# Taking temporaries and output pieces by the age of their store, and four lower halves on VectorE

## The chip, the cores and the metric

The kernel runs on one core of a Trainium2 chip. The metric is the device time of one execution in microseconds: the median of 3 runs of the kernel before is 1347.68 us (1347.32 to 1349.24).

## The reference

Chunked attention, then two feed-forward experts, all in float32. The second expert is the part that the change touches: `h = x @ w_in` with 4608 tokens, 512 to 2048 columns, then SiLU, then `@ w_out` back to 512.

```python
def _moe2_ref(x, w_in, w_out):
    h = x @ w_in
    g = h * (1.0 / (1.0 + np.exp(-h)))
    return (g @ w_out).astype(np.float32)

x = attention(q, k, v)          # chunks of 64, softmax, 8 heads
x = _moe_ref(x, moe_w_in, moe_w_out, moe_g_ln)   # SoLU and layer norm between two products
return _moe2_ref(x, moe2_w_in, moe2_w_out)
```

## The kernel before

One plan holds the work of all engines: `at(when, fn, ...)` puts a function at due times in us, and `Plan.run` calls the functions in order of due time. A function that yields goes on at its next due time. What is issued in this order stands in the same order in each engine's queue; an instruction that waits holds everything behind it on its engine. All DMAs are issued by SP, in order.

Every float32 product is made of three fp32r products of a high part and a lower part (`PASSES`): the high part is a rounded copy, the lower part is the value less that copy.

Both products of the second expert are done by blocks of 2 x 2 with seven products of half size (`SEVEN`: p1, p6, p2, p7, p5, p4, p3) in place of eight, and sums around them.

*Way in* (lines 478 to 630). A unit `u` is 768 tokens by two pieces of 128 hidden columns; the units are worked in 24 pairs, 14 products of 6 matmuls a pair, due `PA = 14 * SL = 14.59` us apart with `SL = 1.042`. The outputs are copied or summed out of PSUM into temporaries (`tmp`, 128 x 384): `c_p1` takes one, `c_u2` (line 598), `c_u3` (602) and `c22` (612) take one each, and the blocks c11, c22, c21 and c12 end in the pieces of p1, c22, u3 and u2. Each passes through SiLU on ScalarE and goes to DRAM (`gd`) by `g_store`. There are nine temporaries; `take()` hands them out in rotation. In one pair starting at x, unit i (0 or 1), the due times are y = x + (i + 1) SL + 0.05 for `c_p1`, y + 2 SL for `c_u2`, y + 6 SL for `c_u3`, y + 8 SL for `c22`; the stores are due at y + 4 SL + 0.8 (c11), y + 8 SL + 1.2 (c22), y + 10 SL + 1.2 (c21) and y + 12 SL + 1.2 (c12). A PSUM bank that a sum reads is written again by a later product, so a late sum stops TensorE: p7 goes into the bank that `c_u2` reads, p3 into the one that `c22` reads.

Beside it weights are prepared: `conv_a` (lines 159, 162), `conv_b` and `w2_mix` (250, 254 on GpSimd, stored at 257) make the second weight's pieces; `w2t` and `w2o` are loads of finished weights; `raw_load` (513) loads the input `ry` of the next 768 tokens, four loads of 384 KB, into five places, and `s_split` (548) cuts it into halves.

*Way out* (lines 633 to 735). Token pairs `v` of 256 tokens, 18 of them, seven products of 24 matmuls each. `g_load` (676) brings the rows from `gd` into one of two sets, `g_sum` (683) makes the sums, `g_split` makes the high part on ScalarE (694) and the lower part (696) on VectorE for the first four products and on GpSimd for the last three, into a ring of six places. Pairs 0 and 1 run interleaved (`turn`). `g_load(2, i)` overwrites the set that pair 0 read. Outputs are summed in six pieces (`ob`, line 721) and stored (734); `o_take` hands the pieces out by a table, in pairs from 2 on by a rotation of six.

Of the kernel before, what the change touches and what calls it, by code (L numbers as in the profile page):

```python
# [9 lines left out]
F32 = mybir.dt.float32  # L10
# [5 lines left out]
ALU = mybir.AluOpType  # L16
# [8 lines left out]
class Plan:  # L25
# [9 lines left out]
    def at(self, when, fn, *args):  # L35
        lead = self.lead.get((fn.__name__, *(a for a in args if isinstance(a, int))))
        when = [x / 100 for x in lead] if lead else [when] if isinstance(when, float) else when
        self.items.append((when, fn, args))
# [13 lines left out]
def chunk_attention_moe_moe(ctx: ExitStack, tc: tile.TileContext, q, k, v, w_in, w_out, g_ln, w2_in, w2_out, out):  # L52
    nc = tc.nc
# [54 lines left out]
    for i in range(2 * KD):  # L108
        kk, c = i % KD, i // KD * CW
# [3 lines left out]
    for m in range(KD):  # L113
        for a in range(2):
            src = w_out[a * 512:(a + 1) * 512, m * 128:(m + 1) * 128].rearrange("(k p) f -> p k f", p=128)
# [370 lines left out]
    wt, tu, raw_y, sy, bank, tmp, c_t = {}, [], {}, {}, {}, [], {}  # L486
# [65 lines left out]
        tmp.extend(t[:, i, 0:HW] for i in range(n))  # L552

    def take():
        tmp.append(tmp.pop(0))
        return tmp[-1]

    PLACE = {"p1": "x", "p2": "x", "p6": "y", "p7": "y", "p5": "w", "p3": "w", "p4": "v"}

# [25 lines left out]
    def g_store(u, half, low, c):  # L585
        p, j = divmod(u, NF)
        if p == NGR - 1:
            j = NF - 2 - j // 2 * 2 + j % 2
        t = GT * p + GT // 2 * half
        nc.sync.dma_start(out=gd[t:t + GT // 2, :, j + NF * low, :].rearrange("t p c -> p t c"), in_=c.rearrange("p (t c) -> p t c", c=128))  # L590

    def c_p1(u):
        c_t[u, "p1"] = c = take()
        nc.scalar.activation(out=c, in_=bank[u, "x"], func=AF.Copy)

    def c_u2(u):
        c_t[u, "u2"] = c = take()
        nc.vector.tensor_tensor(out=c, in0=bank[u, "y"], in1=c_t[u, "p1"], op=ALU.add)  # L598

    def c_u3(u):  # L600
        c_t[u, "u3"] = c = take()
        nc.vector.tensor_tensor(out=c, in0=bank[u, "y"], in1=c_t[u, "u2"], op=ALU.add)

    def c11(u):
        c = c_t[u, "p1"]
        nc.scalar.activation(out=c, in_=bank[u, "x"], func=AF.Silu)
        yield
        g_store(u, 0, 0, c)

    def c22(u):  # L610
        c = take()
        nc.vector.tensor_tensor(out=c, in0=bank[u, "w"], in1=c_t[u, "u3"], op=ALU.add)  # L612
        yield
        nc.scalar.activation(out=c, in_=c, func=AF.Silu)
        yield
        g_store(u, 1, 1, c)

    def c21(u):
        c = c_t[u, "u3"]
        nc.vector.tensor_tensor(out=c, in0=bank[u, "v"], in1=c, op=ALU.add)  # L620
        yield
        nc.scalar.activation(out=c, in_=c, func=AF.Silu)
        yield
        g_store(u, 0, 1, c)
# [9 lines left out]


    NP = TT // 2
    wo2, wu, ring, raw_g, ob, takes, o_t = {}, [], [], {}, [], [], {}

    def w2o_load(tag, bufs, n):

# [46 lines left out]
    def turn(v, o):  # L687

        return 7 * v + o if v > 1 else ((0, 1, 3, 5, 7, 9, 11), (2, 4, 6, 8, 10, 12, 13))[v][o]

    def g_split(v, o):
        src = raw_g[v % 2, G_FROM[SEVEN[o]]]
        dst = ring[turn(v, o) % 6]
        nc.scalar.activation(out=dst[:, 0], in_=src, func=AF.Copy)  # L694
        yield
        (nc.gpsimd if o > 3 else nc.vector).tensor_tensor(out=dst[:, 1], in0=src, in1=dst[:, 0].bitcast(F32), op=ALU.subtract)  # L696

    def out_product(v, o):
        acc, start = place(1000 + v, SEVEN[o], 256)
# [5 lines left out]

    def o_take(v, name):

        if v < 2:
            n = {"p1": (0, 2), "u2": (1, 3), "u3": (4, 0), "c22": (5, 2)}[name][v]
        else:  # L710
            n = (1, 4, 5, 2, 0, 3)[len(takes) % 6]
            takes.append(n)
        o_t[v, name] = ob[n]
        return ob[n]

    def o_p1(v):
        nc.scalar.activation(out=o_take(v, "p1"), in_=bank[1000 + v, "x"], func=AF.Copy)  # L717

    def o_sum(v, name, src, with_, new):
        c = o_take(v, name) if new else o_t[v, with_]  # L720
        nc.vector.tensor_tensor(out=c, in0=bank[1000 + v, src], in1=o_t[v, with_], op=ALU.add)  # L721
        if name[0] == "c":
            yield
            o_store(v, int(name[1]) - 1, int(name[2]) - 1, c)

    def o_c11(v):
        c = o_t[v, "p1"]
        nc.scalar.activation(out=c, in_=bank[1000 + v, "x"], func=AF.Copy)
        yield
        o_store(v, 0, 0, c)  # L730

    def o_store(v, i, n, c):
        b, tt = divmod(2 * v + i, BT)
        nc.sync.dma_start(out=out.rearrange("(b s) f -> b s f", b=B)[2 * tt:2 * tt + 2, b * CH:(b + 1) * CH, 256 * n:256 * n + 256], in_=c)


    plan = Plan(LEAD)
# [11 lines left out]
    for i in range(2 * KD):  # L749
        at((-70.0 if i < 4 else -69.0) + 0.1 * i, conv_load, i)  # L750
        x = -31.0 + 2.6 * i
# [11 lines left out]
    for t in range(TT):  # L763
        x = T[t]
# [22 lines left out]
        if t >= BT:  # L787
            x, (b, m) = T[t], divmod(t - BT, BT)
            y = (11.7, 16.9, 19.8)
            if t + 2 == TT:  # L790
                y = (11.7, L + 9.0, L + 11.8)
            elif t + 1 == TT:
                y = (12.0, 15.0, 17.8)
# [3 lines left out]
        x = T[t]  # L797
        for _ in range(CONV[t] if nxt < N1 else 0):
            at(x - 13.5, conv_load, nxt)
            x = T[t] + (3.6 if nxt == 18 else 0.0)  # L800
# [4 lines left out]
            else:  # L805
                at(x + 5.2, conv_c, nxt, side(nxt))
                if nxt % 2:
                    y = 122.2 if nxt == 17 else x + 5.3
# [6 lines left out]
    for m in range(KD):  # L815
        x = XO + 5.44 * m
# [5 lines left out]
    PA = 14 * SL  # L822
    BUFS = {"kT": 1, "pT": 1, "qT": 1, "e": 1, "xs": 1, "wi": 2 * KD, "wo": 4}
    UNITS = {"qT": 1, "e": 1, "wo": 4}
    for when, tags in (
# [5 lines left out]
        for i, tag in enumerate(tags):  # L831
            n = UNITS.get(tag, 2)
# [13 lines left out]
    for n in range(NGR * NF // 2):  # L846
        x = XA + PA * n
        p, jj = divmod(n, NF // 2)
        for i in range(2):
            u = 2 * n + i  # L850
            for o, name in enumerate(SEVEN):
                at(x + (2 * o + i) * SL, product, u, name)
            y = x + (i + 1) * SL + 0.05
            at(y, c_p1, u)
            at(y + 2 * SL, c_u2, u)
            at((y + 4 * SL, y + 4 * SL + 0.8), c11, u)
            at(y + 6 * SL, c_u3, u)
            at([y + 8 * SL + d for d in (0.0, 0.6, 1.2)], c22, u)
            at([y + 10 * SL + d for d in (0.0, 0.6, 1.2)], c21, u)
            at([y + 12 * SL + d for d in (0.0, 0.6, 1.2)], c12, u)  # L860
        if jj == 0:
            x -= PA
            on = ((ACT, DVE), (ACT, DVE), (ACT, DVE), (ACT, DVE), (ACT, POOL), (ACT, DVE), (ACT, POOL))
            for o, (hi_on, lo_on) in enumerate(on):
                y = x + (2 * o + 2) * SL + 0.2
                if p == 0:
                    y = XO + 1.0 + 2.0 * o if o < 5 else XA + 0.3 + 1.2 * o - 6.0
                at((y, y + 1.0), s_split, p, o, hi_on, lo_on)
                if o in (0, 2):
                    at(y + 1.1, raw_t, p, 2 if o == 0 else 3)  # L870
            if p + 1 < NGR:
                y = x + PA * (2.7 if p == 0 else 1.5)
                for i, q4 in enumerate((1, 0, 2, 3)):
                    at(y + 0.7 * i, raw_load, p + 1, q4)
                at(x + PA * (3.75 if p % 2 == 0 else 2.8), raw_t, p + 1, 0)
                at(x + PA * (3.9 if p % 2 == 0 else 2.93), raw_t, p + 1, 1)

    before = XA - 6.3
    for i in range(K2):
        n = N1 + i  # L880
        x = XA + PA * (8 * (i // 6) + ((0.7, 1.4, 2.4, 4.3, 5.4, 6.1) if i < 6 else (0.4, 1.1, 2.2, 2.85, 5.4, 6.1))[i % 6])
# [10 lines left out]
    for when, step, tags in (  # L892
# [5 lines left out]
        for tag in tags:  # L898
            n = UNITS.get(tag, 2)
# [13 lines left out]
    for vp in range(NP):  # L913
        x = XB + 7 * SB * vp
        for i in (2, 3, 0, 1):
            at(XB + FIRST_LOADS[vp][i] if vp < 3 else x - 11 * SB + 0.1 * i, g_load, vp, i)
        for n in range(4):
            at(XB + FIRST_SUMS[vp][n] if vp < 2 else x + (-6.2, -5.7, -3.2, -0.9)[n] * SB, g_sum, vp, n)
        ends = []
        for o in range(7):  # L920
            n = turn(vp, o)
            y = XB + (FIRST_SPLITS[n] if n < 14 else (n - 4.7) * SB)
            at((y, y + 1.25), g_split, vp, o)
            at(XB + n * SB, out_product, vp, o)
            ends.append(XB + n * SB + SB)
        d = 0.6 if vp == NP - 1 else 3.4
        at(ends[0], o_p1, vp)
        at(ends[1], o_sum, vp, "u2", "y", "p1", 1)
        at((ends[2], ends[2] + d), o_c11, vp)
        at(ends[3], o_sum, vp, "u3", "y", "u2", 1)  # L930
        at((ends[4], ends[4] + d), o_sum, vp, "c22", "w", "u3", 1)
        at((ends[5], ends[5] + d), o_sum, vp, "c21", "v", "u3", 0)
        at((ends[6], ends[6] + d), o_sum, vp, "c12", "w", "u2", 0)
# [161 lines left out]
```

## Time and profile before

| | |
|---|---|
| median of 3 runs | 1347.68 us |
| the profiled execution | 1346.99 us, span 1345.2 us |
| busy: PE, DVE, ACT, POOL | 95%, 67%, 45%, 42% of the span |
| way in of the second expert on PE | 589.9 to 965.3 us |
| way out on PE | 965.3 us to the end |
| mean granted TensorE clock | 0.988 |
| `gd<-tmp` stores (192 KB) | 192 |

PE is the matrix engine, PEld its weight load, DVE is VectorE, ACT ScalarE, POOL GpSimd, SP the engine that issues DMAs. Times in the rows are us from the start of the span. A bracket at the end of a row is the idle time of the engine before it, and who ended it. A row with a count merges instructions that follow each other.

### The profile page before, as it was taken

To read this page: it belongs to the slowest core of one execution; us is meant where nothing else is said; L and a number is where in the kernel's file an instruction comes from. 1 tells how busy PE (TensorE), PEld (TensorE's weight loads), DVE (VectorE), ACT (ScalarE), POOL (GpSimd) and SP (SyncE) were. 2 spreads that over 40 slices of the span, in tenths; PEclk is the share of its full clock that TensorE was granted. 3 is DMA by queue.
4 is the path that set the end of the run, shared out by engine and by line. 5 is a ranking of instruction groups with operands and counts; after the bars stand their busy time and mean duration, and the time that the engine had idled before them with its cause. 6 is when DMAs were issued, how large, how long until landed. Compare 5 with 4: busy or idle time off the path is not lost. (4 is left out here: it accounts for less than half of the span.)

```text
span 1345.2 us, 22475 instructions
## 1 busy us (share of the span) xinstructions
PE 1271.6 (95%) x8400; PEld 1162.0 (86%) x8400; DVE 898.2 (67%) x1383; ACT 609.7 (45%) x991; POOL 567.1 (42%) x454
## 2 busy tenths in 40 slices
PE   3789999999999999898999999998989999999998
PEld 2578887887888888798999999998989999999997
DVE  7799776878888878434656656562657666666661
ACT  5686544545544555432544445342333443443341
POOL 4443113331222332222554556351166666666662
PEclk9999999999999999999999999999989999999999
DMA  9574456555564651958677566759873443443420
GB/s 200 94 138 87 76 121 149 141 113 148 134 132 111 160 146 49 340 185 269 200 222 216 181 218 206 218 181 308 282 267 133 137 132 127 135 136 123 134 91 29
DMA packets 330846, 217.51 MB, mean 162 GB/s; under 512 B 187248, under 2 KB 288624, under 8 KB 330736
## 3 DMA queue, kind: packets, MB, share of 16 engines
q1 hardware_dynamic: 330736, 216.07, 57.0%
q8 instruction: 66, 1.08, 0.3%
q14 instruction: 44, 0.36, 0.1%
HBM read 130.03 MB, written 85.98 MB: 161 GB/s over the span
## 5 line engine op out<-in xcount | busy, mean ns | idle before, releaser
L703 PE MATMUL h<-w2o,gs 128*128 128x256 f32 x2160 | 269.4, 286 | 2.5 <-DVE gs L696 2.0
L582 PE MATMUL h<-y1s,w2t 128*128 128x384 f32 x1440 | 261.6, 337 | 9.9 <-DVE tmp L598 9.2
L703 PEld LDWEIGHTS h<-w2o,gs 128*128 128x128 f32 x2160 | 265.8, 194 | 3.1 <-DVE gs L696 2.2
L582 PEld LDWEIGHTS h<-y1s,w2t 128*128 128x128 f32 x1440 | 252.4, 189 | 11.8 <-DVE tmp L598 10.4
L409 PE MATMUL h<-wi,xs 128*128 128x512 f32 x864 | 216.9, 400 | 6.4 <-DVE u L426 3.4
L468 PE MATMUL yp<-lnT,wo 128*128 128x512 f32 x864 | 212.1, 396 | 0.7 <-ACT ys L473 0.7
L409 PEld LDWEIGHTS h<-wi,xs 128*128 128x128 f32 x864 | 159.4, 190 | 45.8 <-issue 3.2
L468 PEld LDWEIGHTS yp<-lnT,wo 128*128 128x128 f32 x864 | 159.1, 188 | 38.6 <-issue 5.0
L694 ACT ACTIVATE gs<-g 128x1024 fp32r<-128x1024 f32 x117 | 123.5, 1058 | 150.8 <-PE h L703 76.6
L696 POOL TENSOR_TENSOR gs<-g,gs 128x1024 fp32r<-128x1024 f32 x54 | 147.0, 2727 | 48.5 <-ACT gs L694 45.2
L696 DVE TENSOR_TENSOR gs<-g,gs 128x1024 fp32r<-128x1024 f32 x63 | 107.3, 1706 | 32.3 <-ACT gs L694 31.3
L582 PE MATMUL hw<-y1s,w2t 128*128 128x384 f32 x576 | 111.6, 343 | 6.8 <-DVE tmp L612 6.8
L703 PE MATMUL hw<-w2o,gs 128*128 128x256 f32 x864 | 109.2, 282 | 3.5 <-DMA w2o<-w2od 3.5
L582 PEld LDWEIGHTS hw<-y1s,w2t 128*128 128x128 f32 x576 | 103.3, 193 | 9.1 <-DVE tmp L612 9.1
L703 PEld LDWEIGHTS hw<-w2o,gs 128*128 128x128 f32 x864 | 105.5, 191 | 3.9 <-DMA w2o<-w2od 3.9
L436 POOL TENSOR_TENSOR st<-st,nhalf 128x1 f32<-128x1 f32 x36 | 21.2, 589 | 178.0 <-DVE st L434 178.0
L239 POOL TENSOR_TENSOR cv<-cv 128x256 f32<-128x256 f32 x64 | 46.2, 738 | 96.8 <-DVE cv L209 95.5
L358 POOL TENSOR_TENSOR e<-e,sm 128x512 f32<-128x512 f32 x36 | 42.1, 1168 | 89.7 <-DVE sm L356 85.2
L393 DVE TENSOR_TENSOR lnT<-tp,lnT 128x512 fp32r<-128x512 f32 x72 | 49.3, 685 | 38.8 <-ACT lnT L384 38.1
L683 POOL TENSOR_TENSOR g<-g,g0x 128x1024 f32<-128x1024 f32 x18 | 43.4, 2413 | 74.3 <-DVE gs L696 74.3
L384 ACT ACTIVATE lnT<-tp 128x512 fp32r<-128x512 f32 x72 | 42.9, 596 | 59.5 <-PE tp L454 59.4
L598 DVE TENSOR_TENSOR tmp<-h,tmp 128x384 f32<-128x384 f32 x48 | 26.6, 556 | 63.1 <-DMA gd<-tmp 34.7
(116 smaller groups left out, 1798.8 us busy)
## 6 DMA issues: line engine op xcount, KB each, us to landing
gd<-tmp SPq DMA_DIRECT2D x192, 192.0 KB
g<-gd SPq DMA_DIRECT2D x72, 512.0 KB
w2d<-cv_m SPq DMA_DIRECT2D x56, 256.0 KB
w2t<-w2d SPq DMA_DIRECT2D x56, 256.0 KB
w2od<-y1s SPq DMA_DIRECT2D x56, 256.0 KB
w2o<-w2od SPq DMA_DIRECT2D x27, 512.0 KB
st_w<-in_moe_w_out_dram SPq DMA_DIRECT2D x24, 512.0 KB
vt<-in_v_dram SPq DMA_DIRECT2D x36, 256.0 KB
```

The lines of the kernel that those rows point to most:

```text
L239: nc.gpsimd.tensor_tensor(out=out, in0=in0, in1=in1, op=op)
L358: nc.gpsimd.tensor_tensor(out=e, in0=e, in1=sm.to_broadcast([128, HP, 2, CH]), op=ALU.mult)
L384: nc.scalar.activation(out=hi, in_=src, func=AF.Copy)
L393: nc.vector.tensor_tensor(out=lo, in0=src, in1=hi.bitcast(F32), op=ALU.subtract)
L409: nc.tensor.matmul(h_t[t][:, n, :], xs[:, a, kk, :], wi[b][kk][:, n * 512:(n + 1) * 512], start=(kk == 0 and i == 0), stop=(kk == KD - 1 a ...
L468: nc.tensor.matmul(yps[b, m], wo[a][f // 4][:, f % 4, 128 * m:128 * (m + 1)], lnT[b][c][:, f, :], start=(f == 0 and i == 0), stop=(f == K1 ...
L582: nc.tensor.matmul(acc, w[:, a, kk, :], t[:, i, c, :], start=start and kk == 0 and n == 0, stop=kk == 1 and n == 2, skip_group_check=not s ...
L598: nc.vector.tensor_tensor(out=c, in0=bank[u, "y"], in1=c_t[u, "p1"], op=ALU.add)
L683: on.tensor_tensor(out=out, in0=in0, in1=in1, op=op_)
L694: nc.scalar.activation(out=dst[:, 0], in_=src, func=AF.Copy)
L696: (nc.gpsimd if o > 3 else nc.vector).tensor_tensor(out=dst[:, 1], in0=src, in1=dst[:, 0].bitcast(F32), op=ALU.subtract)
L703: nc.tensor.matmul(acc, g[:, a, f, :], wo2[o, f][:, c, :], start=start and f == 0 and i == 0, stop=f == NF - 1 and i == 2, skip_group_chec ...
```

## The change

`take` gives the piece that has been free longest, and `g_store` puts a piece at the end of the list when its store is issued. `o_take` and `o_store` do the same with the output pieces. In `g_split` of token pairs 0 and 1 the lower parts of the fifth and sixth product are made on VectorE. The loads of the second 768 tokens' input are due half a `PA` earlier (2.2 for 2.7). The second stage of the output functions is due 5.0 us instead of 3.4 after the product's end for token pairs 0 to 2.

```diff
     def take():
-        tmp.append(tmp.pop(0))
-        return tmp[-1]
+
+        return tmp.pop(0)
@@ g_store
         nc.sync.dma_start(out=gd[t:t + GT // 2, :, j + NF * low, :].rearrange("t p c -> p t c"), in_=c.rearrange("p (t c) -> p t c", c=128))
+        tmp.append(c)
@@ g_split
-        (nc.gpsimd if o > 3 else nc.vector).tensor_tensor(out=dst[:, 1], in0=src, in1=dst[:, 0].bitcast(F32), op=ALU.subtract)
+        (nc.gpsimd if o > (3 if v > 1 else 5) else nc.vector).tensor_tensor(out=dst[:, 1], in0=src, in1=dst[:, 0].bitcast(F32), op=ALU.subtract)
@@ o_take
-        if v < 2:
-            n = {"p1": (0, 2), "u2": (1, 3), "u3": (4, 0), "c22": (5, 2)}[name][v]
-        else:
-            n = (1, 4, 5, 2, 0, 3)[len(takes) % 6]
-            takes.append(n)
-        o_t[v, name] = ob[n]
-        return ob[n]
+        o_t[v, name] = c = ob.pop(0)
+        return c
@@ o_store
+        ob.append(c)
@@ the input loads of the way in
-                y = x + PA * (2.7 if p == 0 else 1.5)
+                y = x + PA * (2.2 if p == 0 else 1.5)
@@ the output functions of the way out
-        d = 0.6 if vp == NP - 1 else 3.4
+        d = 0.6 if vp == NP - 1 else 3.4 if vp > 2 else 5.0
```

Which piece is used is seen on SP, in the stores around the last weight store before the way out (pair 21's last six stores are those behind the `w2od` row, the even unit's first in each kind: c22, c21, c12; 5651 and 5577 are the two `cv_s` tiles of two pieces each, 5578 the `st_w` tile, 5574 to 5576 single pieces). Before:

```order
L257 DMA w2od_77<-y1s_5570 128x512
L590 DMA gd_79<-tmp_5651 128x3x128 x2
L646 DMA w2o_8634<-w2od_77 128x1024
L590 DMA gd_79<-tmp_5577 128x3x128 x2
L590 DMA gd_79<-tmp_5575 128x3x128
L646 DMA w2o_8686<-w2od_77 128x1024
L590 DMA gd_79<-tmp_5576 128x3x128
```

and the next pair's takes by `c_u2`, `c_u3` and `c22` on VectorE, before:

```order
L598 TENSOR_TENSOR tmp_5574<-h2_8698,tmp_5578 128x384
L598 TENSOR_TENSOR tmp_5575<-h2_8707,tmp_5578 128x384
L602 TENSOR_TENSOR tmp_5576<-h2_8698,tmp_5574 128x384
L602 TENSOR_TENSOR tmp_5577<-h2_8707,tmp_5575 128x384
L612 TENSOR_TENSOR tmp_5577<-hw_5652,tmp_5576 128x384
L612 TENSOR_TENSOR tmp_5651<-hw_5652,tmp_5577 128x384
```

In the changed kernel the same six stores on SP:

```order
L257 DMA w2od_77<-y1s_5570 128x512
L590 DMA gd_79<-tmp_5574 128x3x128
L590 DMA gd_79<-tmp_5651 128x3x128
L647 DMA w2o_8634<-w2od_77 128x1024
L590 DMA gd_79<-tmp_5651 128x3x128
L590 DMA gd_79<-tmp_5576 128x3x128
L590 DMA gd_79<-tmp_5575 128x3x128
L647 DMA w2o_8686<-w2od_77 128x1024
L590 DMA gd_79<-tmp_5577 128x3x128
```

and the same takes:

```order
L599 TENSOR_TENSOR tmp_5577<-h2_8698,tmp_5578 128x384
L599 TENSOR_TENSOR tmp_5574<-h2_8707,tmp_5578 128x384
L603 TENSOR_TENSOR tmp_5651<-h2_8698,tmp_5577 128x384
L603 TENSOR_TENSOR tmp_5651<-h2_8707,tmp_5574 128x384
L613 TENSOR_TENSOR tmp_5576<-hw_5652,tmp_5651 128x384
L613 TENSOR_TENSOR tmp_5575<-hw_5652,tmp_5651 128x384
```

The second `c_u2` took the piece of the fifth of the six stores and now takes that of the first.

On SP in pairs 1 and 2 of the way in the loads of `ry` move ahead of stores and weight loads:

```order
 L590 DMA gd<-tmp 128x3x128
+L513 DMA ry<-y1d 128x2x384
+L495 DMA w2t<-w2d 128x512
+L513 DMA ry<-y1d 128x2x384 x3
+L495 DMA w2t<-w2d 128x512
+L590 DMA gd<-tmp 128x3x128 x2
 L495 DMA w2t<-w2d 128x512 x2
```

The four loads stand in front of pair 1's first two stores, where they stood between its later ones.

On VectorE, at the start of the way out, from the sums of token pair 1 to the first sum of token pair 2. Before:

```order
L683 TENSOR_TENSOR g_8983<-g_8879,g_8878 128x1024
L696 TENSOR_TENSOR gs<-g_8983,gs 128x1024
L696 TENSOR_TENSOR gs<-g_8982,gs 128x1024
L721 TENSOR_TENSOR ob<-h_9084,ob 128x256
L696 TENSOR_TENSOR gs<-g_8878,gs 128x1024
L721 TENSOR_TENSOR ob<-h_8991,ob 128x256
L683 TENSOR_TENSOR g_8443<-g_8443 128x1024
```

And of the change:

```order
L684 TENSOR_TENSOR g_8983<-g_8879,g_8878 128x1024
L697 TENSOR_TENSOR gs<-g_8983,gs 128x1024
L697 TENSOR_TENSOR gs<-g_8982,gs 128x1024
L697 TENSOR_TENSOR gs<-g_8443,gs 128x1024
L717 TENSOR_TENSOR ob<-h_9084,ob 128x256
L697 TENSOR_TENSOR gs<-g_8878,gs 128x1024
L697 TENSOR_TENSOR gs<-g_8443,gs 128x1024
L717 TENSOR_TENSOR ob<-h_8991,ob 128x256
L697 TENSOR_TENSOR gs<-g_8879,gs 128x1024
L684 TENSOR_TENSOR g_8443<-g_8443 128x1024
```

Three of the four moved halves are seen, two ahead of a sum of the output each; the fourth stands a few rows on.

## Rows read from the trace of the kernel before

**Rows 1.** Waits of PE from 589 us: engine, line, waited for: us, times, longest.

```profile
PE h L582 <- DVE tmp L598: 9.2, 3, 4.9
PE hw L582 <- DVE tmp L612: 6.8, 5, 2.1
```

**Rows 2.** Timeline of PE, way in: start us, us, what xcount [idle before <-releaser].

```profile
604.51 6.41 PE L582 MATMUL h<-y1s,w2t 128*128 128x384 f32 x36
...
642.21 8.48 PE L582 MATMUL h<-y1s,w2t 128*128 128x384 f32 x48
...
730.91 8.49 PE L582 MATMUL h<-y1s,w2t 128*128 128x384 f32 x48
...
745.53 8.54 PE L582 MATMUL h<-y1s,w2t 128*128 128x384 f32 x48
...
925.37 7.45 PE L582 MATMUL h<-y1s,w2t 128*128 128x384 f32 x42
...
947.00 8.48 PE L582 MATMUL h<-y1s,w2t 128*128 128x384 f32 x48
...
965.27 11.86 PE L703 MATMUL h<-w2o,gs 128*128 128x256 f32 x96
```

**Rows 3.** Timeline of PE, way out.

```profile
980.03 11.33 PE L703 MATMUL h<-w2o,gs 128*128 128x256 f32 x70 [2.04 <-DVE gs L696]
...
1009.08 0.62 PE L703 MATMUL hw<-w2o,gs 128*128 128x256 f32 x3 [2.64 <-DMA w2o<-w2od]
...
1037.16 11.65 PE L703 MATMUL h<-w2o,gs 128*128 128x256 f32 x96
...
1057.25 11.65 PE L703 MATMUL h<-w2o,gs 128*128 128x256 f32 x96
```

**Rows 4.** Timeline of DVE, way in.

```profile
612.74 1.02 DVE L598 TENSOR_TENSOR tmp<-h,tmp 128x384 f32<-128x384 f32 x2 [5.81 <-DMA gd<-tmp]
...
632.17 0.56 DVE L598 TENSOR_TENSOR tmp<-h,tmp 128x384 f32<-128x384 f32 x1 [4.82 <-DMA gd<-tmp]
635.27 0.59 DVE L159 TENSOR_SCALAR cv<-st_w 128x512 int32<-128x512 int32 x1 [2.55 <-POOL y1s L254]
...
937.09 0.56 DVE L598 TENSOR_TENSOR tmp<-h,tmp 128x384 f32<-128x384 f32 x1 [7.78 <-DMA gd<-tmp]
...
953.12 0.56 DVE L598 TENSOR_TENSOR tmp<-h,tmp 128x384 f32<-128x384 f32 x1 [2.18 <-DMA gd<-tmp]
...
958.52 2.70 DVE L696 TENSOR_TENSOR gs<-g0x,gs 128x1024 fp32r<-128x1024 f32 x1
```

**Rows 5.** Timeline of SP, issues of DMAs around pair 21's last stores.

```profile
924.20 0.43 SPq L646 DMA_DIRECT2D w2o<-w2od  x1
...
928.40 0.96 SPq L590 DMA_DIRECT2D gd<-tmp  x2
...
930.30 1.88 SPq L590 DMA_DIRECT2D gd<-tmp  x3
```

**Rows 6.** Windows: stretch, busy us of PE, PEld, DVE, ACT, POOL, PEclk, DMA share, GB/s.

```profile
921.00:942.00 21.00, 16.12 (x83) 15.80 (x82) 5.39 (x10) 4.89 (x10) 2.27 (x4) 0.84 1.02 327
942.00:973.60 31.60, 29.52 (x182) 29.20 (x181) 19.58 (x23) 13.11 (x22) 4.81 (x2) 0.95 0.86 275
973.60:981.00 7.40, 5.00 (x36) 4.59 (x35) 6.22 (x5) 4.62 (x7) 2.42 (x1) 0.89 0.91 367
981.00:1009.00 28.00, 24.58 (x185) 24.17 (x183) 13.80 (x11) 8.46 (x9) 20.93 (x8) 0.91 0.75 250
```

**Rows 7.** Timeline of DVE, way out.

```profile
973.65 1.23 DVE L683 TENSOR_TENSOR g<-g,g 128x1024 f32<-128x1024 f32 x1 [1.73 <-DMA g<-gd]
...
977.47 3.64 DVE L696 TENSOR_TENSOR gs<-g,gs 128x1024 fp32r<-128x1024 f32 x2 [1.13 <-ACT gs L694]
```

**Rows 8.** Timeline of POOL, end of the way in.

```profile
957.75 2.39 POOL L683 TENSOR_TENSOR g<-g,g0x 128x1024 f32<-128x1024 f32 x1 [29.79 <-DVE gs L696]
```

**Rows 9.** Timeline of POOL, start of the way out.

```profile
983.52 16.22 POOL L696 TENSOR_TENSOR gs<-g,gs 128x1024 fp32r<-128x1024 f32 x6
```

More of the change, by code (lines that the diff above doesn't have):

```diff
@@ L636, in chunk_attention_moe_moe @@
     NP = TT // 2
-    wo2, wu, ring, raw_g, ob, takes, o_t = {}, [], [], {}, [], [], {}
+    wo2, wu, ring, raw_g, ob, o_t = {}, [], [], {}, [], {}
     def w2o_load(tag, bufs, n):
```

## The prediction

> **What bounds the kernel now.** I read the waits of TensorE from the start of the second expert's way in, then TensorE in order of time, then the engines that it waited for.
>
> The waits [rows 1] name VectorE: 9.2 us before products that need the sum of line 598 (`c_u2`), 6.8 before those that need line 612 (`c22`). In order of time [rows 2] an undisturbed pair of units lasts 745.53 - 730.91 = 14.62 us. Three places are longer. Pairs 1 and 2 take 642.21 - 604.51 = 37.70 for 29.24: 8.46 lost. Pair 22 takes 947.00 - 925.37 = 21.63: 7.01 lost. Pair 23 takes 965.27 - 947.00 = 18.27: 3.65 lost. The losses hold each wait and the matmuls that ran slower behind it. On the way out a token pair lasts 1057.25 - 1037.16 = 20.09 [rows 3]; the first three take 1037.16 - 965.27 = 71.89 for 60.27: 11.62 lost, around two waits, 2.04 at 980.03 for a lower half from VectorE and 2.64 at 1009.08 for a weight transfer. The rest of both stages runs close to its period, and waits of other engines there cost nothing. So 8.46 + 7.01 + 3.65 + 11.62 = 30.74 us is the most that this change can give back.
>
> **Temporaries by age.** Nine pieces serve four takes a unit, and a unit's pieces come free in another order than they were taken: `p1` first, `u2` last. With PA = 14.59 and SL = 1.042 the due times give the age of the store at the next take. In rotation the odd unit's `u2` takes a piece whose `c12` store is due 4.0 us earlier (due x + 14.80, taken x + 18.81), `u3` of the even unit one of 6.1; in pair 1 `u2` gets one of 1.9. By age the smallest is 8.2, mostly 10.3; what gets younger falls from 14.4 to 10.3 and 18.6 to 14.4.
>
> VectorE shows what the young ones cost [rows 4]: it sat 5.81 us at 612.74, 4.82 at 632.17 and 7.78 at 937.09, each time until a store of a piece had landed. The third has its stores in the queue's rows [rows 5]: the six of pair 21 go out late, two at 928.40, three from 930.30; the awaited one is the third of these, issued by 932.18 and landed by 937.09, so 4.9 to 6.8 us in the queue. In the changed order the same take gets the first of the six, issued at 928.40. At that age it would land at 933.3 to 935.2, and with 0.56 for the sum TensorE, which needs it half a pair in at 925.37 + 7.3 = 932.7, would still wait 1.2 to 3.1 us. But SP issued nearly nothing from 924.63 to 928.40, so the queue in front of the first is shorter than in front of the fifth by the weight load and the stores between. I take nothing as left, with 3.1 for the range. Pair 22's 7.0 go; its following takes have stores from 930.30 on against needs from 936 on.
>
> Pairs 1 and 2: the takes that waited get pieces that are unused yet or whose stores are due 8.2 earlier. One of the three waits there is not a temporary's: line 159 at 635.27 waited 2.55 for GpSimd, which waited for its own weight pieces to be stored, with VectorE's sums queued behind. The four loads of y1, due 0.5 PA = 7.3 us earlier, leave that stretch. They are 4 x 384 KB = 1.57 MB, at 327 GB/s [rows 6] 4.8 us of the queue. Behind them stand now weight loads of a later pair and pair 1's stores of `p1`, whose pieces are next taken 10.7 us later: nothing waits, and 4.8 us is the price if that cover were gone. I count all 8.46; 5 if GpSimd's part stays.
>
> Pair 23: the wait for line 612 was a chain, 2.18 us for a store at 953.12, then the lower half of 958.52 at 2.70 us where VectorE takes 1.23 for one of this size [rows 4, 7], with a GpSimd subtraction of 2.39 us started at 957.75 beside it [rows 8]. Without the first, the sum of line 612 is ready 2.2 us earlier, against a wait of 2.1. I count 3.65, and 0 at the other end.
>
> So the way in ends 8.46 + 7.01 + 3.65 = 19.1 us earlier.
>
> **What is late next.** The way out's second input rows come by DMA. VectorE's sum at 973.65 waited for them [rows 7], the product 6.4 us later at 980.03 for VectorE [rows 3]. In the changed kernel TensorE is there 19.1 us earlier; are the rows? The queue ran full from 921 to 942 (share 1.02, 327 GB/s), and from 942 to 973.6 at 0.86 and 275 GB/s [rows 6]: 8.69 MB. Pairs 1 and 2 shift all of it by 8.46. Of the other 10.7 us only what the queue had idle can be had: 8.69 MB take 26.6 us at 327 GB/s, 23.7 at the 367 of 973.6 to 981, for 31.6 now. The rows land 5.0 to 7.9 us earlier, 4.4 by the share (0.86 x 31.6 = 27.2). I take 6.5, since small stores and large loads mix as between both rates. The product at 980 comes 8.5 + 6.5 = 15.0 earlier; 4 us of the way in's gain turn into a longer wait there. The matmuls behind it ran slow already (70 in 11.33 us; at the period's rate, 168 in 20.09, they take 8.4), so I count no more of that.
>
> **Lower halves on VectorE.** Four subtractions leave GpSimd's run of six, 16.22 us from 983.52, 2.7 each [rows 9]. The third token pair's first row load (`g_load(2, 2)`) overwrites the tile that the first of them reads, so it goes at 983.52 + 2.7 = 986.2, and the last weight pieces stand behind it and its three fellows on SP. VectorE is done with its second half before them at 977.47 + 3.64 = 981.11 [rows 7]; a moved one takes 1.23 to 2.70: done by 982.3 to 983.8, the load 2.1 to 3.6 earlier. The later loads gain less, since the next half waits behind a sum that needs TensorE. Of the 2.64 us at 1009 I take 2.0; bounds 0 and 3.5. Price on VectorE: 4 x 1.23 = 4.9, at most 4 x 2.70 = 10.8; from 981 to 1009 it is busy 13.8 of 28 us [rows 6], so 14.2 are free.
>
> The row at 958.52 shows a held VectorE instruction: GpSimd's ended at 960.14, VectorE's at 961.22, about one free duration later. The Trainium skill's page "SBUF — State Buffer", section "SBUF: two separate sides", gives the rule: the port pair that both engines share is an exclusive lock, held for the whole instruction, and the other one blocks. By that rule the trace agrees, and it speaks against the moved halves: the last rival below is what it would do here.
>
> **Output pieces and stores.** Six pieces by age: the youngest store at a take is 6.5 us old by the due times instead of 5.2. Twelve stores of pairs 0 to 2 are due 1.6 us later and let weight loads pass on SP; they end long before the kernel does. Worth 0 to 0.5; counted as 0.
>
> **Sum.** 8.5 + 6.5 + 2.0 = 17.0. The profiled execution took 1346.99 us (span 1345.2 and 1.8 around it), 0.7 under the median shown: 1346.99 - 17.0 = 1330.0.
>
> **Rivals.**
> - *All waits go.* The transfers keep up: 1346.99 - 30.7 = 1316.2. For it: the queue's share is only 0.75 from 981 to 1009. Against: it is full before, and loads have to land before a chain of sums. 0.12.
> - *Transfers set the way out.* The queue closes no gap, and way in's last two pairs give nothing: only 8.5 stays, 1338.5. For it: share 1.02. Against: 0.86 behind it. 0.20.
> - *The pieces are no older where it counts.* Stores go out late as at 928.40, whatever the due time, since SP stood behind something else. Pairs 1 and 2 lose half their gain, pair 22 all: 1346.99 - 4 = 1343. Against: it takes the first of six instead of the fifth. 0.06. That nothing moves at all (within 0.2%, 2.7 us, what a measurement of this kernel can tell from no change): 0.03.
> - *VectorE's halves hold up the sums.* In the first two token pairs each moved half stands ahead of a sum that frees a bank of TensorE's. Held for a whole GpSimd half, 2.7, each takes 2.7 + 1.23 = 3.9, four 15.7; with TensorE waiting for all of it, and 11.33 - 8.4 = 2.9 for the slower matmuls behind, that is 18.6 on a gain of 15.0: 1350.6, slower. It decides once more than the 14.2 us free on VectorE are taken, which needs all four held; with only two halves left on GpSimd there it is unlikely. 0.03.
>
> **Numbers.** The forecast has 0.56, with 1323 to 1336 its own range. The range to 1320 takes in part of the first rival, to 1339 the second. Faster by over 0.2%: 0.56 + 0.12 + 0.20 + 0.05 = 0.93; within 0.04; slower 0.03.
>
> **What would show it.** VectorE's waits for a landed store in front of lines 598 and 602 are gone; pairs 1, 2, 22 and 23 last 14.6 each; the way out's second half at its first wait is late by 5 to 7 us instead of 2, with the DMA share near 1.0 before it; the third token pair's first row load goes before GpSimd's first half; the last weight wait shrinks below 1 us. Wrong would be a store still ending a VectorE wait in pairs 1, 2 or 22, or TensorE waiting for sums of the output behind a moved half. If the wait at the product of 980 vanishes, the transfer term is wrong and the time is nearer 1320.

## The result and the profile after

The changed kernel takes 1329.55 us (median of 4 runs, 1328.85 to 1330.23), the kernel before timed beside it 1347.97 (1347.32 to 1349.24): a ratio of 0.9862, interval 0.9845 to 0.9879. The forecast was 1330.0. The profiled execution took 1330.23 us, span 1328.4, so the spans differ by 1345.2 - 1328.4 = 16.8; the medians differ by 18.4. Of the kernel with the temporaries alone, below, two of five runs (3181.55 and 4885.99 us), and of the kernel before one of eleven timed beside it (2080.74), were in a slower state and are left out.

The waits of TensorE from the start of the second expert's way in; columns as in [rows 1].

```profile
PE hw L582 <- DVE tmp L613: 7.8, 5, 4.1
PE h L704 <- ACT gs L695: 2.0, 1, 2.0
PE h L704 <- DVE gs L697: 2.0, 1, 2.0
PE h L582 <- ACT tmp L595: 0.6, 1, 0.6
PE hw L704 <- DMA w2o<-w2od: 0.3, 1, 0.3
```

The 9.2 us in front of products that need `c_u2` [rows 1] are gone. The wait for the sum of `c22` (now line 613) is larger than its 6.8, and one wait holds more than half of it. TensorE in order of time, way in:

```profile
587.75 8.51 PE L582 MATMUL h<-y1s,w2t 128*128 128x384 f32 x48
...
602.34 8.49 PE L582 MATMUL h<-y1s,w2t 128*128 128x384 f32 x48
...
616.96 8.54 PE L582 MATMUL h<-y1s,w2t 128*128 128x384 f32 x48
...
633.74 4.21 PE L582 MATMUL hw<-y1s,w2t 128*128 128x384 f32 x12 [4.06 <-DVE tmp L613]
637.75 9.32 PE L582 MATMUL h<-y1s,w2t 128*128 128x384 f32 x48
...
921.64 8.52 PE L582 MATMUL h<-y1s,w2t 128*128 128x384 f32 x48
...
936.30 8.48 PE L582 MATMUL h<-y1s,w2t 128*128 128x384 f32 x48
...
949.98 2.36 PE L582 MATMUL hw<-y1s,w2t 128*128 128x384 f32 x12 [1.03 <-DVE tmp L613]
952.18 11.66 PE L704 MATMUL h<-w2o,gs 128*128 128x256 f32 x96
```

And way out:

```profile
965.87 0.50 PE L704 MATMUL h<-w2o,gs 128*128 128x256 f32 x2 [2.03 <-ACT gs L695]
968.39 11.11 PE L704 MATMUL h<-w2o,gs 128*128 128x256 f32 x70 [2.02 <-DVE gs L697]
...
993.37 1.26 PE L704 MATMUL hw<-w2o,gs 128*128 128x256 f32 x6 [0.28 <-DMA w2o<-w2od]
...
1020.29 11.65 PE L704 MATMUL h<-w2o,gs 128*128 128x256 f32 x96
```

From the starts of the pairs in these rows and in [rows 2, 3], with the way in's own start (589.9 before):

| stretch, us | before | after | difference |
|---|---|---|---|
| start of the way in | 589.9 | 587.7 | -2.2 |
| pairs 1 and 2 | 37.70 | 35.41 | -2.3 |
| pairs 3 to 21 | 283.2 | 283.9 | +0.7 |
| pair 22 | 21.63 | 14.66 | -7.0 |
| pair 23 | 18.27 | 15.88 | -2.4 |
| way out, first 21 products | 71.89 | 68.11 | -3.8 |
| the rest, to the start of TensorE's last matmul | 301.2 | 301.2 | 0 |

The first line is no effect of the change, which touches nothing ahead of the way in: in thirteen profiled executions of kernels that are alike up to there the way in began anywhere between 587.7 and 591.5. Differences of stages within one execution are read more finely than whole times for that reason. Stages scatter too: in five kernels that are alike up to the end of pair 21, the changed one and four of the experiments, pairs 1 and 2 took 33.88 to 35.41, so the 35.41 here is the longest; in four alike to the end of the way in, pair 23 took 15.46 to 17.57.

Why pair 2 waits is seen in three engines. SP, GpSimd and VectorE, in that order:

```profile
622.87 0.92 SPq L257 DMA_DIRECT2D w2od<-y1s  x2
```

```profile
627.78 0.40 POOL L250 CAST y1s<-cv 128x256 fp32r<-128x256 f32 x1 [7.87 <-DMA w2od<-y1s]
```

```profile
629.02 0.59 DVE L159 TENSOR_SCALAR cv<-st_w 128x512 int32<-128x512 int32 x1 [7.07 <-POOL y1s L254]
...
630.40 1.01 DVE L603 TENSOR_TENSOR tmp<-h,tmp 128x384 f32<-128x384 f32 x2
```

GpSimd cannot make its next weight piece until the store issued at 622.87 has landed; VectorE stands at line 159 until GpSimd has gone on, 7.07 us where it was 2.55 [rows 4]; the two sums of line 603 behind it wait with it. In the kernel before, the start of pair 2 on TensorE and the same store on SP were these:

```profile
623.41 7.48 PE L582 MATMUL h<-y1s,w2t 128*128 128x384 f32 x42
```

```profile
628.59 0.86 SPq L257 DMA_DIRECT2D w2od<-y1s  x2
```

Counted from the way in's start, VectorE came to line 159 8.6 us earlier than before (621.95 - 587.7 against 632.72 - 589.9), since its own waits for temporaries had gone. The store was issued only 3.5 us earlier (622.87 - 587.7 against 628.59 - 589.9).

### The profile page after: what moved, and what is told of

It reads as the page before. It is cut to its first block, busy times and chain, and to the rows that moved or that the text cites. A ratio compares the mean times of both kernels' runs of the same rounds, so it can differ in the third digit from the quotient of the medians.

```text
span 1328.4 us, 22474 instructions
## 1 busy us (share of the span) xinstructions
PE 1266.9 (95%) x8400; PEld 1159.2 (87%) x8400; DVE 903.0 (68%) x1387; ACT 609.9 (46%) x991; POOL 558.9 (42%) x450
## 5 line engine op out<-in xcount | busy, mean ns | idle before, releaser
L697 POOL TENSOR_TENSOR gs<-g,gs 128x1024 fp32r<-128x1024 f32 x50 | 139.0, 2781 | 51.8 <-ACT gs L695 48.9
L697 DVE TENSOR_TENSOR gs<-g,gs 128x1024 fp32r<-128x1024 f32 x67 | 112.7, 1687 | 31.2 <-ACT gs L695 30.2
L615 ACT ACTIVATE tmp<-tmp 128x384 f32<-128x384 f32 x48 | 24.6, 526 | 88.7 <-DVE tmp L613 88.5
```

Source lines behind the costliest of these rows:

```text
L697: (nc.gpsimd if o > (3 if v > 1 else 5) else nc.vector).tensor_tensor(out=dst[:, 1], in0=src, in1=dst[:, 0].bitcast(F32), op=ALU.subtract)
```

## The experiments

Each kernel was timed against the kernel before on the same chip; the time of the changed kernel, 1329.55, stands for comparison. The kernel before took 1346.3 to 1348.0 beside them, so two kernels timed apart are compared by their ratios. Stage lengths are from the starts of TensorE's products in each run's one profiled execution.

**The temporaries alone, and all but them.** The first kernel is the one before with `take` and `g_store` of the change; the second is the changed kernel without them.

```diff
     def take():
-        tmp.append(tmp.pop(0))
-        return tmp[-1]
+        return tmp.pop(0)
```

> The kernel before with temporaries by age alone. Theory A (the age of the pieces carries the way in's end): pairs 22 and 23 fall from 21.6 and 18.3 to 14.7 and about 15.9 us as in the change, pairs 1 and 2 give 2 to 4 us, the way out's first three token pairs keep 70 to 72 us with GpSimd's six halves; 1335 to 1340 in all. Rival B (the halves on VectorE and the moved stores carry the change): 1344 to 1348, since the earlier end of the way in turns into a longer wait at the way out's first products.

> The change with the temporaries in rotation again. Theory A: pairs 22 and 23 are back at 21 and 18 us, the way out keeps its 68 us; 1339 to 1345. Rival B: under 1335.

Measured: 1337.33 (median of three runs; ratio 0.9937, 0.9904 to 0.9970) and 1339.67 (0.9944, 0.9928 to 0.9960). With the temporaries alone pair 22 takes 14.61, pair 23 16.64, pairs 1 and 2 35.18; without them 20.15, 18.15 and 36.80. The waits of TensorE without them:

```profile
PE h L582 <- DVE tmp L598: 7.3, 3, 3.8
PE hw L582 <- DVE tmp L612: 6.1, 4, 1.8
```

So the age of the pieces takes away pair 22's wait and all waits at `c_u2`, and does so alone. It does not give pairs 1 and 2 their 8.46. With the temporaries alone the way out's first 21 products take 74.69, 2.8 more than before: 1.3 more in the first six, at the waits where the forecast had it, and 1.8 more in products 11 to 13 (counted from 0), which reach the last weights sooner. Theory A had 70 to 72 there. The other edits bring the 74.69 to 68.11. Without the temporaries these products take 65.30, where theory A had 68: the temporaries cost the way out 74.69 - 71.89 = 2.8 without the other edits and 68.11 - 65.30 = 2.8 with them, and the other edits win 6.6 either way.

**The input loads.**

```diff
-                y = x + PA * (2.2 if p == 0 else 1.5)
+                y = x + PA * (2.7 if p == 0 else 1.5)
```

> The change with the four input loads due at 2.7 again. As the prediction had it, the loads come back into the stretch in which GpSimd waits for its weight stores: TensorE's 4.06 us wait in pair 2 grows to 6 to 8 and the time to 1332 to 1334. Rival C (the early loads fill the queue just in front of those stores and make the wait): the wait falls below 2 us, 1325 to 1328. Rival D (the queue is full either way): same within 1 us.

Measured: 1331.92 (0.9888, 0.9866 to 0.9910). Pairs 1 and 2 take 35.59 against 35.41, and the wait is there in the same form. TensorE, then VectorE:

```profile
634.51 4.21 PE L582 MATMUL hw<-y1s,w2t 128*128 128x384 f32 x12 [4.25 <-DVE tmp L613]
```

```profile
629.79 0.59 DVE L159 TENSOR_SCALAR cv<-st_w 128x512 int32<-128x512 int32 x1 [7.26 <-POOL y1s L254]
```

With the loads back in the stretch the wait is as long as in the changed kernel within 0.2 us, and not 6 to 8. Moving the loads helps pairs 1 and 2 by 0.2 us here, and by 1.7 at most if the shortest of the five kernels alike there, 33.88, is set against 35.59. Pair 11 took 17.84 instead of 15.75, the largest difference of a stage. That pair took 18.40 in a later kernel with the loads at their new place, and the ratios' intervals overlap, so no worth of this edit is shown.

**VectorE's order in pair 2.** If VectorE waits at line 159 with finished work behind it, it is enough to put that line later. Two kernels make the third weight piece due 2.95 and 2.70 pairs after the start instead of 2.40.

```diff
-        ... ((0.7, 1.4, 2.4, 4.3, 5.4, 6.1) if i < 6 ...
+        ... ((0.7, 1.4, 2.95, 4.3, 5.4, 6.1) if i < 6 ...
```

> Against the changed kernel, whose median is 1329.6 us: the third weight piece of the way in is made half a pair later (due 2.95 instead of 2.4 periods), so VectorE's line 159 stands behind the sums of pair 2 instead of in front of them. Theory V: the 4.06 us that TensorE still waits before a product of pair 2 is VectorE standing in its own order at line 159, which waits for GpSimd's weight piece, which waits for its store. Then that wait falls below 1 us, pairs 1 and 2 take at most 32 us instead of 35.4, and the whole kernel 1324 to 1327. Rival T: the stretch is short of transfers in any order, and another sum or a row load is late in its place: pairs 1 and 2 stay at 34 to 36, the kernel at 1328 to 1331. Rival M: the delay moves on, pairs 3 to 21 grow by 2 us or more from 283.9, and the kernel stays at 1328 to 1331.

> The third weight piece due 2.70 instead of 2.40 periods: VectorE's line 159 stands behind the first sum of line 613 of pair 2 instead of two sums ahead of it, so it still runs near 629, when GpSimd's piece is out, and not half a pair later as with 2.95. Theory V (the wait in pair 2 is VectorE's order, and what pair 3 lost with 2.95 was the piece being late): pairs 1 and 2 take 29.3 to 31 us instead of 35.4, pairs 3 to 21 stay at 283 to 285, the kernel 1324 to 1327. Rival K (the weight arithmetic and GpSimd's work collide wherever they meet, and give it back in pair 3): pairs 1 and 2 at 29.3 to 31, pairs 3 to 21 at 287 or more, 1328 to 1332.

Measured with 2.95: 1332.68 (0.9898, 0.9880 to 0.9916); with 2.70: 1328.57 (0.9866, 0.9847 to 0.9884). In both pairs 1 and 2 take 29.26, so nothing is left to wait for: theory V on the cause holds. Its times, 1324 to 1327, did not come. With 2.95 pairs 3 to 21 grew by 4.9, more than rival M had, and with 2.70 their length and the time lie where rival K had them. With 2.95 all of it is given back, with 2.70 more than half. With 2.95 pair 3 takes 19.87, where the changed kernel has 15.60, pairs 3 to 21 288.8 and pair 22 16.50. VectorE and GpSimd with 2.95, in pair 3:

```profile
635.85 2.28 DVE L176 SCALAR_TENSOR_TENSOR cv<-st_w,cv 128x512 int32<-128x512 int32 x1 [1.25 <-ACT cv L164]
...
639.68 2.56 DVE L548 TENSOR_TENSOR y1s<-ry,y1s 128x768 fp32r<-128x768 f32 x1
```

```profile
635.74 1.85 POOL L519 TENSOR_TENSOR ry<-ry 128x768 f32<-128x768 f32 x1
...
639.17 2.25 POOL L519 TENSOR_TENSOR ry<-ry 128x768 f32<-128x768 f32 x1
```

Line 176 takes 2.28 us here and 0.76 at 631.33 in the changed kernel, line 548 2.56 against 0.95 at 642.44. Each ends 0.5 to 0.8 us after the GpSimd subtraction that began before it. TensorE waits 2.70 us in pair 3, until 642.77, for a sum of line 599 that stands right behind the second. With 2.70 line 159 runs where it ran before, but behind the first sum. VectorE:

```profile
628.36 0.56 DVE L613 TENSOR_TENSOR tmp<-hw,tmp 128x384 f32<-128x384 f32 x1 [1.54 <-PE hw L582]
628.84 0.57 DVE L159 TENSOR_SCALAR cv<-st_w 128x512 int32<-128x512 int32 x1
```

Pair 3 takes 16.91, 1.3 more than in the changed kernel; pairs 3 to 21 take 287.3, of which pair 11's 18.40 is 2.7 more. Whether that pair is late through the edit stays open for this kernel alone; the last experiment has it at 15.53.

**Are transfers the first wait of the way out?** Three weight loads ahead of token pair 1's last two row loads go behind them. (They are 512 KB each; the expectation has 256.)

```diff
-        (XB - 6.4, 1.5, ("wi", "wi", "wi", "wi", "xs", "vt", "vt")),
+        (XB + 2.5, 0.9, ("wi", "wi", "wi", "wi", "xs", "vt", "vt")),
```

> Against the changed kernel, 1329.6: three weight loads of the way out, 256 KB each, that stand on SP in front of the last two row loads of token pair 1 go behind them; the bytes are the same. Theory T: transfers set the way out's first waits (2.03 us at 965.87 and 2.02 at 968.39): the rows that VectorE's sum at 962.03 waited 3.24 us for land 2.5 to 5 us earlier, the two waits together fall below 1.5 us, and the kernel takes 1326 to 1328. Rival C: the order of VectorE's and ScalarE's own halves sets them: the sum is earlier, the two waits stay above 3 us together, 1329 to 1331. Rival W: the weights moved back are late for their products, a wait for a weight load of over 1 us appears before 980, and the kernel takes 1330 to 1333.

Measured: 1329.36 (0.9863, 0.9842 to 0.9884), by its median no faster. Its profiled execution is the fastest of its four, so only the stages speak. The changed kernel, VectorE, at the sum that needs these rows:

```profile
962.03 1.23 DVE L684 TENSOR_TENSOR g<-g,g 128x1024 f32<-128x1024 f32 x1 [3.24 <-DMA g<-gd]
...
965.85 4.75 DVE L697 TENSOR_TENSOR gs<-g,gs 128x1024 fp32r<-128x1024 f32 x3 [1.12 <-ACT gs L695]
```

With the loads behind, VectorE and then TensorE:

```profile
958.18 1.23 DVE L684 TENSOR_TENSOR g<-g,g 128x1024 f32<-128x1024 f32 x1 [1.88 <-DMA g<-gd]
...
962.00 4.77 DVE L697 TENSOR_TENSOR gs<-g,gs 128x1024 fp32r<-128x1024 f32 x3 [1.12 <-ACT gs L695]
```

```profile
949.69 11.66 PE L704 MATMUL h<-w2o,gs 128*128 128x256 f32 x96
962.02 0.50 PE L704 MATMUL h<-w2o,gs 128*128 128x256 f32 x2 [0.67 <-ACT gs L695]
964.55 9.99 PE L704 MATMUL h<-w2o,gs 128*128 128x256 f32 x70 [2.03 <-DVE gs L697]
```

Counted from the way out's start the sum runs at 958.18 - 949.69 = 8.49 instead of 962.03 - 952.18 = 9.85, and TensorE's first wait shrinks by the same 1.36, from 2.03 to 0.67. The second keeps its length, since the half that ends it comes 2.5 us after the one that ends the first, in both; VectorE starts on that half when ScalarE has made its high part. So transfers set when both products can start, and the chain of sum, high part and lower part sets the length of the second wait. Theories T and C are right on one each, and the two waits together, 2.70, lie between what they expected. The two kernels with both repairs, below, have first waits of 0.4 and 0.6 too. The matmuls behind ran faster too, 70 in 9.99 us instead of 11.11.

**Halves, output pieces, stores.** Three kernels take from the changed one the halves on VectorE, the output edits (pieces and stores), and the stores alone.

```diff
-        (nc.gpsimd if o > (3 if v > 1 else 5) else nc.vector)...
+        (nc.gpsimd if o > 3 else nc.vector)...
```

```diff
-        d = 0.6 if vp == NP - 1 else 3.4 if vp > 2 else 5.0
+        d = 0.6 if vp == NP - 1 else 3.4
```

> The change with the lower halves of token pairs 0 and 1 on GpSimd again. Theory A: the first row load of token pair 2 goes 2 to 4 us later, the wait for the last weight pieces is back at 2 to 3.5 us and slower matmuls behind it: 1332 to 1336. Rival E (the shorter wait for weights came from the moved output stores): 1329 to 1330.5.

> The changed kernel with the output pieces in their old fixed order and the stores of token pairs 0 to 2 due 3.4 us after their product again. By the prediction these edits are worth 0 to 0.5 us: 1329 to 1331, the last weight wait below 1 us, products 11 to 13 of the way out in 9.4 to 10.5. Rival: it is these edits that shortened the wait for the last weights, beside VectorE's halves: products 11 to 13 take 11.5 us or more, the last weight wait is 1.5 us or more, 1331 to 1334.

> The changed kernel (1329.6 us) with only the due times of the twelve output stores put back; the output pieces stay by age. On SP two weight loads then stand behind an output store again. Theory S: these stores are what held the last weight load: the last weight wait is 1.5 us or more, products 11 to 13 of the way out take 12 to 13.5 us instead of 9.4, the kernel 1331 to 1334. Rival P: the pieces by age did it: the last weight wait stays under 1 us, products 11 to 13 at 9.4 to 10.5, the kernel 1329 to 1331.

Measured: 1333.28 (0.9899, 0.9866 to 0.9932), 1333.18 (0.9896, 0.9878 to 0.9913) and 1332.62 (0.9894, 0.9876 to 0.9912). The intervals of all three touch that of the change, so here too the stages speak. Products 11 to 13 of the way out, where the last weights are awaited, take 14.13 before, 9.43 in the changed kernel, 12.41 without the halves, 13.09 without the output edits, 13.58 without the stores. With the temporaries alone it was 15.96. From there the output edits take 15.96 - 12.41 = 3.55, the halves 15.96 - 13.09 = 2.87, both 6.53: they add to within 0.1 us. Other kernels with both edits, those with the loads back and with the piece at 2.95 or 2.70, take 9.40 to 10.33, clear of the 12.41 to 13.58. Of the output edits it is the twelve due times, as theory S had it. SP in the changed kernel, and then with the old due times:

```profile
982.10 0.54 SPq L730 DMA_DIRECT2D out_dram<-ob  x1
982.68 4.05 SPq L647 DMA_DIRECT2D w2o<-w2od  x2
986.83 0.52 SPq L730 DMA_DIRECT2D out_dram<-ob  x1
987.41 3.39 SPq L677 DMA_DIRECT2D g<-gd  x1
```

```profile
983.80 3.73 SPq L647 DMA_DIRECT2D w2o<-w2od  x2
987.64 0.53 SPq L730 DMA_DIRECT2D out_dram<-ob  x1
988.27 3.07 SPq L647 DMA_DIRECT2D w2o<-w2od  x1
```

TensorE with the old due times:

```profile
998.07 0.63 PE L704 MATMUL hw<-w2o,gs 128*128 128x256 f32 x3 [2.64 <-DMA w2o<-w2od]
```

In both a store stands in front of two weight loads; with the old due times one more, of 128 KB, stands in front of the last, and that is enough. The issue of that load takes 3.07 us where one took 0.43 [rows 5], and ends at 991.34, 38.2 us after this way out's start at 953.1. In the changed kernel the last weight goes out before that store, its issue ends at 982.68 + 4.05 = 986.73, 34.6 after the start, and TensorE waits 0.28 for it. The slow issue is then that of a row load, at 987.41, which is not awaited so soon.

**Both repairs.** The weight loads behind the rows, with the piece due at 2.95 and at 2.70.

> The late weight piece and the three weight loads behind the rows, together. If pairs 1 and 2 hang on VectorE's order and the way out's first waits on transfers, the gains add: 1321 to 1324. If the queue of transfers swallows what pairs 1 and 2 give back, as the prediction had it for pairs 22 and 23: 1324 to 1327. If neither edit helps: 1328 or more.

> The piece due at 2.70 and the three weight loads of the way out behind the rows. If theory V holds for the piece, its gain and the 2.9 us that the way out's first 21 products gained alone add up: 1321 to 1324. If the piece's gain is given back in pair 3: 1326 to 1330.

Measured: 1328.37 (0.9866, 0.9852 to 0.9881) and 1323.99 (0.9833, 0.9816 to 0.9851; runs from 1323.1 to 1326.5). The first takes 29.26 for pairs 1 and 2, 19.69 for pair 3 and 66.24 for the first 21 products: pair 3 gives back what the piece won, as with 2.95 alone. The second is the fastest kernel here. Its median is 5.6 us under that of the changed one; by the ratios it is 3.9 us, and their intervals just overlap, while they are clear of each other between the two kernels here. It takes 29.26 for pairs 1 and 2, 284.8 for pairs 3 to 21 with pair 3 at 16.81 and pair 11 at 15.53, and 65.96 for the first 21 products, so by the stages the gains add, as theory V had it. Its TensorE:

```profile
646.90 2.36 PE L582 MATMUL hw<-y1s,w2t 128*128 128x384 f32 x12 [1.97 <-DVE tmp L613]
...
986.13 1.26 PE L704 MATMUL hw<-w2o,gs 128*128 128x256 f32 x6 [1.97 <-DMA w2o<-w2od]
```

It waits for the last weight again, 1.97 us, and 1.97 in pair 3 at the line that it waited for in pair 2: what is left has gone to the next in line.

## Why the prediction came out, step by step

The total was right, 1330.0 for 1329.55, by luck: three of its terms were not. Way in: 19.1 forecast; 2.3 - 0.7 + 7.0 + 2.4 = 11.0 measured. Way out: 4.1 lost and 2.0 won forecast, -2.1 together; 3.8 won measured, which the four kernels with and without the temporaries and the other edits split into 2.8 lost and 6.6 won. The way in's start gave 2.2, which is scatter of the two profiled executions and no part of the change. So -8.1, +5.9 and +2.2 cancelled.

*Pairs 1 and 2, the step that failed.* "The four loads of y1 ... leave that stretch. ... I count all 8.46; 5 if GpSimd's part stays." It stayed, and the rest was not 5 but 2.3 (3.8 in the best of the five kernels alike there): pair 1 is clean (616.96 - 602.34 = 14.62), and pair 2 takes 20.79, longer than the 18.8 of before. Two waits of one engine in sequence, here for a temporary's store and for GpSimd, are not two terms of a sum. When the first goes, the engine stands sooner at the second, whose end, counted from the start of pair 2, hardly moves: VectorE is through with its wait at 629.02 - 616.96 = 12.06, before at 635.27 - 623.41 = 11.86, and 2.55 became 7.07. The loads were not its cause: with them back the wait is 7.26. The 0.7 in pairs 3 to 21 is pair 3, whose first 48 matmuls, behind the long wait, took 9.32 for 8.48 before [rows 2].

*Pair 22.* 7.0 forecast, 6.97 measured, and the runs with and without the temporaries give it to them. The 3.1 that was kept for the range did not come: the first of the six stores was early enough, and only just. VectorE at that take, after:

```profile
928.21 0.56 DVE L599 TENSOR_TENSOR tmp<-h,tmp 128x384 f32<-128x384 f32 x1 [2.64 <-DMA gd<-tmp]
```

A store still ends a wait of VectorE in pair 22, which the prediction named as a sign of being wrong. But the sum is done at 928.77, and TensorE needs it half a pair in, at 921.64 + 7.3 = 928.9. By the list of its waits it waits for none of line 599. VectorE's waits for landed stores at this line were 34.7 us in 17 in the trace of before and are 5.6 us in four.

*Pair 23.* 3.65 forecast, 2.39 measured, and 0.7 to 2.8 by the four kernels alike there. The chain's second link outlived the first. A lower half stands in front of the sum on VectorE and takes 2.08 us, beside a GpSimd operation. VectorE, GpSimd:

```profile
947.38 2.08 DVE L697 TENSOR_TENSOR gs<-g0x,gs 128x1024 fp32r<-128x1024 f32 x1
```

```profile
945.98 2.40 POOL L684 TENSOR_TENSOR g<-g,g0x 128x1024 f32<-128x1024 f32 x1 [20.82 <-DVE gs L697]
```

The prediction saw the same pair of instructions at 958.52 and then counted as if only the store stood ahead of the sum.

*The way out's first waits.* 4.1 of the way in's gain was to turn into a longer wait, 5 to 7 us instead of 2. The wait came, as two of 4.05 together, and its first part is one for transfers, as the run with the weight loads behind shows; the queue was full ahead of it. Windows of the changed kernel, columns as in [rows 6]:

```profile
921.00:942.00 21.00, 21.00 (x122) 20.94 (x121) 7.54 (x15) 7.02 (x15) 1.14 (x2) 1.00 1.03 344
942.00:961.00 19.00, 17.97 (x127) 17.65 (x126) 14.70 (x15) 8.91 (x14) 4.83 (x2) 1.00 1.07 376
```

The size was off: the way in ended 965.27 - 952.18 = 13.1 earlier and the product of 980.03 came 980.03 - 968.39 = 11.6 earlier, so 1.45 was lost there, beside what the other edits won; the temporaries alone cost the whole of the first 21 products 2.8. With a gain on the way in of 11 instead of 19 there was less to lose: the transfers could give 6.5 us beyond pairs 1 and 2 by the prediction's own working, and pairs 22 and 23 asked for 9.4, 2.9 more. Where the 2.8 falls differs: without the other edits 1.3 in the first six products and 1.8 in 11 to 13; with them 24.29 - 20.35 = 3.9 in the first six, while 11 to 13 get 10.55 - 9.43 = 1.1 shorter.

*The last weights.* 2.0 forecast, 4.7 measured, as 1.8 lost to TensorE's coming sooner, 2.9 won by the halves and 3.55 by the stores. The halves were sized too small: the third token pair's first row load goes at 970.63, 18.45 after the way out's start, against 985.93 - 965.27 = 20.66 before and 977.54 - 954.51 = 23.03 in the changed kernel without them, so 4.6 earlier by their own doing for a forecast of 2.1 to 3.6. What failed is "Worth 0 to 0.5; counted as 0" for the output stores: it asked what the pieces wait for and when the stores end, and not what stands behind each store on SP. There stood the last weight load.

*The rivals.* Pairs 1 and 2 alone as the gain, 1338.5, is out: pair 22's gain reached the end. That all waits go is out by pair 2. That VectorE's halves hold up the output's sums is out: with them the first 21 products are 72.84 - 68.11 = 4.7 shorter, and no wait for line 717 is in TensorE's list. That the pieces are no older where it counts is out by pair 22.

## What to carry to other kernels

When an engine waits twice in a row for different things, ask of the second when its releaser is done by the clock, not how long the wait is: removing the first may only lengthen the second. An engine that waits in order with finished work behind it is cured by moving the waiting instruction behind that work, no further than its releaser needs: a weight piece moved by 0.3 of a pair kept part of the gain where 0.55 gave all of it back. By the whole time this is clear only beside the moved weight loads, 1323.99 against 1328.37. And an edit to due times is priced by what stands behind each moved instruction on its queue: a store that nobody waits for held up a load that everyone waited for.

## What the runs showed of the hardware

TensorE's granted clock after waits. Windows of the changed kernel, behind the 4.06 us wait of pair 2 and behind the two waits of the way out:

```profile
633.74:637.75 4.01, 4.01 (x13) 4.01 (x13) 1.48 (x3) 1.50 (x3) 3.93 (x4) 0.50 0.59 196
...
968.39:979.33 10.94, 10.94 (x70) 10.94 (x71) 6.46 (x7) 3.87 (x4) 4.88 (x2) 0.74 0.53 166
```

And of the fastest kernel, the same 70 matmuls behind waits of 0.62 and 2.04, in 8.64; TensorE, then the window:

```profile
961.93 8.64 PE L704 MATMUL h<-w2o,gs 128*128 128x256 f32 x70 [2.04 <-DVE gs L697]
```

```profile
961.93:970.40 8.47, 8.47 (x70) 8.47 (x71) 7.75 (x7) 3.86 (x4) 4.91 (x2) 1.00 0.90 334
```

Behind the long wait the clock was 0.50, the lower of its two levels (1.2 GHz), and 12 matmuls took 4.21 us instead of 2.24. Behind 2.03 and 2.02 it averaged 0.74, behind 0.62 and 2.04 it stayed at 1.00: 1.4 us less waiting saved 11.11 - 8.64 = 2.5 us more in the matmuls. A wait that is shortened a little can so be worth more than its length. How much more is not fixed by the length alone: with the weight loads moved and the piece left, the waits were 0.67 and 2.03, nearly those of the fastest kernel, and the clock was 0.84 and the 70 matmuls took 9.99.

With the piece at 2.95, two of VectorE's operations with two inputs ended 0.54 and 0.82 us after a GpSimd operation that began first (638.13 after 637.59, 642.24 after 641.42), a little less than the 0.76 and 0.95 that they take free. The Trainium skill's page "SBUF — State Buffer", section "SBUF: two separate sides", says that the port pair shared by VectorE and GpSimd is an exclusive lock, which the instruction that starts first holds to its end; by that rule the trace agrees. The two took 1.5 and 1.6 us longer than in the changed kernel, and pair 3 4.3. No run took that apart.

A DMA issued right behind an output store (128 KB) of the way out's first token pairs took long to issue: 3.07 and 3.39 us in the rows above, and 3.58 of the 4.05 at 982.68, where other issues there take 0.3 to 1.1. The first such store had no such effect (971.05, and a weight load at 971.79 issued in 0.37). What the issue waits for stays open: the profile names no releaser, and no run here took it apart.
